# Two PSUM pools and the place of two groups of transposes in an attention and expert kernel

## The chip, the cores and the metric

The kernel runs on one core of a Trainium2 chip. The metric is the device time of one execution in microseconds (us). The core has five engines that work side by side and hand work to each other by semaphores: PE (matrix products and transposes, whose weight loads are shown apart as PEld), DVE and ACT (elementwise work; only these two empty PSUM here), POOL (elementwise work in SBUF and some DMA issues) and SP (DMA issues).

## The reference

Attention with local and global tokens, then a mixture of eight experts whose routing weights come from Sinkhorn steps. Shapes: 8 batches, 8 heads, 512 local and 32 global tokens, head size 64; D = 512, E = 8, F = 1024, N = 8 x 544 = 4352 rows.

```python
k_all, v_all = concat([k_g, k_l]), concat([v_g, v_l])
out_g = softmax(scale * q_g @ k_all.T) @ v_all              # global rows see everything
s_ll  = where(|i - j| <= 32, scale * q_l @ k_l.T, -1e9)     # local rows see a band ...
a_l   = softmax(concat([scale * q_l @ k_g.T, s_ll]))        # ... and the global keys
out_l = a_l @ v_all
x = concat([out_g, out_l]) as rows of 512
P = exp(x @ w_gate - max);  8 times: P /= rowsum; P /= colsum; P *= N / E
out = sum over e of  P[:, e] * (relu(x @ w1[e]) @ w2[e])
```

## The kernel before

The kernel has three stages. In the first, up to about 341 us, attention is worked off in slots, and the first products (`x @ w1`) of experts 0 to 3 are placed between its steps as fillers. Then come the Sinkhorn steps with the fillers that are left, and from about 376 us on the expert stage, which is not touched.

A unit of attention is a pair of heads of one batch: `HP` = 4 pairs, 8 batches, 32 units. The loop over `s` writes out one slot after the other; slot s works on scores of unit s and finishes unit s - 1. The order within a slot is the order in which the lines are written: every engine takes its own instructions in that order. Slots 0 to 3 are built differently; the loop in question runs from s = 4 to 32. Steps of a slot, with what each puts on the engines:

- `st_B(s, 0..2)`: scores of the eight blocks of unit s, in groups of three, three and two (PE, L299 and L301, tile `sc`); DVE adds the mask and takes the extreme value (L306, tile `ms`); ACT takes the exponential (L309, tile `Pu`).
- `st_N(s, ...)`: DVE takes reciprocals of the sums (L345) and normalises `Pu` (L346); POOL does the same for the columns of the global keys (L350, tile `Pl`).
- `st_D1(s - 1)`: eight transposes of the normalised `Pu` on PE (L357, tile `ptw`), copied to SBUF by DVE (L359, tile `pw`).
- `st_D2(s - 1)`: two transposes of `Pl` on PE (L365), copied by ACT (L367, tile `pg`).
- `st_A(s + 1)`: transposes of the next unit's keys and queries (PE, L273), copied by DVE (L274, `kTe`) and ACT (L283, `qbd`).
- `st_E(s - 1)`: probabilities times values (PE, L378 and L381, tile `po`), evicted from the ninth unit on by ACT (L384, `xT`).
- For global rows, two pairs of heads at a time: `st_G0` (POOL copies into `qgbd`), `st_G1` (PE, L407, tile `sg`; maximum on DVE, L409 and L410; exponential on ACT, L412, tile `Pg`), in the next slot `st_GN` (DVE, L418 and L419: reciprocal and normalisation of `Pg`), `st_G2` (five transposes on PE, L426, copied by ACT, L428, tile `pgs`) and `st_G3` (PE, L440 and L441, tile `pog`; ACT, L445). `st_G1` runs at the end of slots 5 to 8 and of the odd slots from 9 on; `st_GN`, `st_G2` and `st_G3` in the slots 6 to 9 and the even slots from 10 on.
- `f1("a")`, `f1("v")`: one filler each, four matmuls of 128 x 512 (PE, L466, tile `ph`), evicted by ACT (L469) or DVE (L471). `f1("va")` is two of them, the first evicted by DVE.
- `logits` in the slots 5, 9, 13 and so on: small products (PE, L453), copied by DVE (L455).

PSUM is divided into pools: `ps_mm` (two buffers, tag `mm`: fillers and logits), `ps_sc` (two, tag `sc`: scores and `pog`), `ps_po` (one, tag `po`, large enough for `sg`: `po` of `st_E` and `sg` of `st_G1` take turns) and `ps_tr` (two, tag `tr`: all the transposes). A tile waits for the readers of the tile that held its buffer before.

From slot 9 on, a slot before the change runs: D1, GN, G0, two fillers (`"aa"`), B0, D2, G2, B1, two fillers (`"va"`), A, B2, one filler (`"v"`), E, G3, two fillers (`"va"`), N, then in slots without G1 one filler (`"v"`), in some `logits`, and in odd slots G1.

Of the kernel before, what the change touches and what calls it, by code (L numbers as in the profile page):

```python
# [10 lines left out]
FP32 = mybir.dt.float32  # L11
# [12 lines left out]
def kernel(  # L24
# [15 lines left out]
    B, H, Sl, Dh = q_l.shape  # L40
# [3 lines left out]
    P = 128  # L44
# [6 lines left out]
    HP = H // 2  # L51
# [34 lines left out]
    ps_po = pss.enter_context(tc.tile_pool(name="ps_po", bufs=1, space=PSUM))  # L86
# [3 lines left out]
    with tc.tile_pool(name="att_c", bufs=1) as att_c, \  # L90
# [121 lines left out]
        def run(steps):  # L212
            for f in steps:
                f()
# [70 lines left out]
        def st_B(n, part):  # L285
            b, hp = divmod(n, HP)
            qb, kt = qbd[n % 2], kTe[n % NK]
            if part == 0:
                st[n] = dict(Pu=att_wk.tile([P, NHB, SW], FP16, tag="Pu", name="Pu"),
                             mx=att_wk.tile([P, NHB], FP32, tag="mx", name="mx"),  # L290
                             sm=att_wk.tile([P, NHB], FP32, tag="sm", name="sm"))
            d = st[n]
            i0 = 3 * part
            ni = min(3, NHB - i0)
            sc = ps_sc.tile([P, 512], FP32, tag="sc")
            ms = att_wk.tile([P, 3, SW], FP32, tag="ms")
            for ii in range(ni):
                i = i0 + ii
                nc.tensor.matmul(sc[:, SW * ii : SW * ii + KW], qb[:, i, :],  # L299
                                 kt[:, HB * i : HB * i + KW], start=True, stop=True)  # L300
                nc.tensor.matmul(sc[:, SW * ii + KW : SW * (ii + 1)], qb[:, i, :],  # L301
                                 kgT[:, hp, Sg * b : Sg * (b + 1)], start=True, stop=True)
            for ii in range(ni):
                i = i0 + ii
                mi = 0 if i == 0 else (2 if i == NHB - 1 else 1)
                nc.vector.tensor_tensor_reduce(  # L306
                    out=ms[:, ii, :], in0=sc[:, SW * ii : SW * (ii + 1)], in1=mask[:, mi, :],
                    scale=-scale, scalar=BIG, op0=ALU.add, op1=ALU.min, accum_out=d["mx"][:, i : i + 1])
                nc.scalar.activation(out=d["Pu"][:, i, :], in_=ms[:, ii, :], func=AF.Exp, scale=-1.0,  # L309
                                     bias=d["mx"][:, i : i + 1], accum_out=d["sm"][:, i : i + 1])  # L310
# [42 lines left out]
        def st_D1(n):  # L353
            d = st[n]
            ptw = ps_tr.tile([P, NHB, P], FP16, tag="tr")
            for i in range(NHB):
                nc.tensor.transpose(ptw[:, i, :], d["Pu"][:, i, 0:KW], identity)  # L357
            d["pw"] = att_wk.tile([P, NHB, P], FP16, tag="pw", name="pw")
            nc.vector.tensor_copy(out=d["pw"], in_=ptw)  # L359

        def st_D2(n):
            d = st[n]
            pt = ps_tr.tile([P, 2, P], FP16, tag="tr")
            for t in range(2):
                nc.tensor.transpose(pt[:, t, :], d["Pl"][:, 4 * t : 4 * t + 4, :], identity)  # L365
            d["pg"] = att_wk.tile([P, 2, P], FP16, tag="pg", name="pg")
            nc.scalar.copy(out=d["pg"], in_=pt)  # L367

        def st_E(n):
            b, hp = divmod(n, HP)  # L370
            d = st.pop(n)
            vz = vgz[b % 2]
            po = ps_po.tile([P, Sl], FP32, tag="po", name="po")
            for i in range(NHB):
                c = slice(HB * i, HB * (i + 1))
                halves = [(a, slice(HB * a, HB * (a + 1))) for a in range(2)]
                for a, r in halves:
                    nc.tensor.matmul(po[r, c], vab[b % 2][i % 2][:, i // 2, 2 * hp + a, :], d["pw"][:, i, r],  # L378
                                     start=True, stop=False)
                for a, r in halves:  # L380
                    nc.tensor.matmul(po[r, c], vz[:, i % 4, 2 * hp + a, :], d["pg"][:, i // 4, r],  # L381
                                     start=False, stop=True)
            cp = nc.vector.tensor_copy if HP <= n < 2 * HP else nc.scalar.copy
            cp(out=xT[b][:, hp, :], in_=po)  # L384
            if hp == HP - 1:
                nc.sync.dma_start(out=xd[b], in_=xT[b])
# [34 lines left out]
        def st_G2(b, g):  # L421
            Pg = gs[(b, g)][0]
            pt = ps_tr.tile([P, 5, P], FP16, tag="tr")
            for t in range(5):
                c0 = P * t if t < 4 else S - P
                nc.tensor.transpose(pt[:, t, :], Pg[:, c0 : c0 + P], identity)  # L426
            pgs = att_wk.tile([P, 5, P], FP16, tag="pgs", bufs=1)
            nc.scalar.copy(out=pgs, in_=pt)  # L428
            gs[(b, g)] = pgs
# [58 lines left out]
        def f1(engs, **kw):  # L488
            nonlocal n1
            v = 0  # L490
            for eng in engs:
                k, fm = divmod(n1, FT)
                if k < len(fill) and slot >= HP * fill[k][1] + 5:
                    p_l1(*fill[k], fm, eng, **kw)
                    n1 += 1
                    v += 1 if fill[k][1] < B else 0.5
            return v
# [75 lines left out]
        for s in range(HP, NU + 1):  # L573
            slot = s
            b, hp = divmod(s, HP)
            g1 = s in gat
            g23 = s - 1 in gat
            if g1:
                gn = divmod(gat[s], 2)
            if g23:  # L580
                gp = divmod(gat[s - 1], 2)
            if s == HP:
                st_B(s, 0)
                st_D1(s - 1)
                st_D2(s - 1)
                select_v(1, 0, range(2, NJ))
                st_E(s - 1)
                select_v(1, 1, (NJ - 1,))
                slot = s + 1
                va, vb = vab[1]  # L590
                nc.scalar.dma_start(out=vb[0:HB, 0 : NJ - 1], in_=va[HB:P, 0 : NJ - 1])
                nc.scalar.dma_start(out=vb[HB:P, 0 : NJ - 1], in_=va[0:HB, 1:NJ])
                cast_qk(1, 1, gq)
            else:
                if s <= 2 * HP:
                    st_B(s, 0)
                st_D1(s - 1)
                if g23:
                    st_GN(*gp)
            if g1 and s > HP + 1:  # L600
                st_G0(*gn)
            f1("aa")
            if 2 * HP < s < NU:
                st_B(s, 0)
            if s > HP:
                st_D2(s - 1)
            if g23:
                st_G2(*gp)
            if s < NU:
                st_B(s, 1)  # L610
            if s > HP:
                f1("va")
            if s + 1 < NU:
                st_A(s + 1)
            if s < NU:
                st_B(s, 2)
            f1("v")
            if s > HP:
                st_E(s - 1)
            if s == HP + 1:  # L620
                for t, (src, g, dst) in gcast:
                    transpose_g(t, g, dst)
                st_G0(*gn)
            if g23:
                st_G3(*gp)
            if s > HP:
                f1("va")
            if s < NU:
                st_N(s, 0, 6)
                st_N(s, 6, NHB)  # L630
            if s == HP:
                gcast = [(cast_g(x[0], x[1]), x) for x in ((kgf, 1, kgT), (qgf, 0, qgT), (qgf, 1, qgT))]
                load_w1e(3)
            if s > 2 * HP and not g1:
                f1("v")
            if s >= 5 and (s - 5) % HP == 0:
                logits(NJ * ((s - 5) // HP), NJ)
            if g1:
                st_G1(*gn)
            if s < NU and b + 1 < B:  # L640
                if hp == 0:
                    load_qk(b + 1, 0, (nc.sync, nc.sync))
                    load_qk(b + 1, 1, (nc.sync, nc.sync))
                elif hp == 1:
                    cast_qk(b + 1, 0, gq)
                    if b >= NL - 1:
                        load_w1d(b + 1)
                elif hp == 2:
                    vq = load_v(b + 1)
                    run(vq[:3])  # L650
                    cast_qk(b + 1, 1, gq)
                else:
                    run(vq[3:])
# [273 lines left out]
    for fm in range(FT):  # L927
        pool, tag = cyc[fm % 2]
# [10 lines left out]
    for i, (m, e) in enumerate(units):  # L939
        if i == NUN - 1:  # L940
            last_pair(i)
        elif i % 2 == 0:
# [9 lines left out]
            else:  # L952
                n = groups[m][1]
                h = hs[i + 1]
                s = ss[i + 1] = xsp.tile([P, HF, n], FP16, tag="xs", name="sl")
# [55 lines left out]
```

## Time and profile before

| what | value |
|---|---|
| median of 3 runs | 1057.38 us (1055.8 to 1061.52) |
| the profiled execution, its span | 1057.3 us, 1055.5 us |
| busy over the span: PE, PEld, DVE, ACT, POOL | 97%, 66%, 77%, 46%, 13% |
| busy in 95 to 331 us (236 us): PE, PEld, DVE, ACT, POOL | 229.59, 129.50, 180.44, 192.37, 72.70 us |
| busy in 376 to 1055 us (679 us): PE, DVE, ACT | 672.87, 527.60, 201.90 us |
| granted TensorE clock in 95 to 1055 us | 1.00 |

Times are us from the start of the span. A row of a timeline has the start, the duration, the engine, the line, the operation, the tiles written and read, their shapes and a count; what follows in square brackets is idle time of that engine ahead of the row and what ended it. A row of the waits names who waited for whom, the total, the number of times and the longest.

### The profile page before, as it was taken

To read this page: it belongs to the slowest core of one execution; us is meant where nothing else is said; L and a number is where in the kernel's file an instruction comes from. 1 tells how busy PE (TensorE), PEld (TensorE's weight loads), DVE (VectorE), ACT (ScalarE), POOL (GpSimd) and SP (SyncE) were. 2 spreads that over 40 slices of the span, in tenths; PEclk is the share of its full clock that TensorE was granted. 3 is DMA by queue.
4 is the path that set the end of the run, shared out by engine and by line. 5 is a ranking of instruction groups with operands and counts; after the bars stand their busy time and mean duration, and the time that the engine had idled before them with its cause. 6 is when DMAs were issued, how large, how long until landed. Compare 5 with 4: busy or idle time off the path is not lost.

```text
span 1055.5 us, 21693 instructions
## 1 busy us (share of the span) xinstructions
PE 1025.4 (97%) x8854; PEld 700.0 (66%) x8854; DVE 809.6 (77%) x1466; ACT 489.4 (46%) x1248; POOL 132.2 (13%) x215
## 2 busy tenths in 40 slices
PE   7799999999999999999999999999999999999998
PEld 4455555555554466677777777777777777777787
DVE  8587777777776776997877877778777787688685
ACT  7678888787886674222222223223223233132231
POOL 7441423413313002000000000000000000000000
PEclk9899999999999999999999999999999999999999
DMA  9887598987945999935435435335336435535441
GB/s 273 200 193 211 106 261 203 218 239 156 255 130 170 270 275 303 259 106 189 170 112 194 154 140 195 125 141 199 143 117 200 168 117 177 209 100 184 170 165 31
DMA packets 97348, 190.82 MB, mean 181 GB/s; under 512 B 33425, under 2 KB 63585, under 8 KB 84449
## 3 DMA queue, kind: packets, MB, share of 16 engines
q1 hardware_dynamic: 54208, 159.61, 43.6%
q0 software_dynamic: 40432, 20.20, 14.8%
q10 hardware_dynamic: 2608, 9.64, 2.4%
q8 instruction: 69, 1.13, 0.4%
q14 instruction: 31, 0.25, 0.1%
HBM read 157.11 MB, written 53.62 MB: 200 GB/s over the span
## 4 chain that ended last, share of the span: by engine, by line
PE 79%; DVE 9%; ACT 7%; issue 3%; DMA 1%; POOL 0%; ACTq 0%; SPq 0%; DVEq 0%; POOLq 0%
PE m L795 26%; PE ph L752 21%; PE ph L466 15%; PE pm L795 10%; ACT Pu L309 3%; DVE Pu L346 3%; PE ptw L357 1%; DVE h L672 1%; ACT hT L469 1%; PE pt L273 1%; ACT qbd L283 1%; DMA h<-hd 1%; PE po L378 1%; PE sc L299 1%; DVE m L409 1%
## 5 line engine op out<-in xcount | busy, mean ns | idle before, releaser
L754 ACT ACTIVATE h<-ph 128x512 f16<-128x512 f32 (+1 forms) x288 | 164.8, 573 | 405.9 <-PE ph L752 397.1
L752 PE MATMUL ph<-xs,w1s 128*128 128x512 f16 (+1 forms) x1152 | 269.4, 367 | 2.0 <-DVE o L811 2.0
L466 PE MATMUL ph<-xT,w1e 128*128 128x512 f16 (+1 forms) x1152 | 257.2, 368 | 0.2
L795 PEld LDWEIGHTS <-h 128*128 128x128 f16 x2144 | 209.8, 98 | 44.1
L795 PE MATMUL m<-w2c,s 128*128 128x256 f16 x1620 | 199.9, 273 | 0.0
L672 DVE TENSOR_TENSOR s<-h 128x1024 f16<-128x1024 f16 (+2 forms) x140 | 122.8, 919 | 91.2 <-ACT h L754 46.8
L795 PEld LDWEIGHTS <-s 128*128 128x128 f16 x1620 | 158.5, 98 | 38.2
L466 PEld LDWEIGHTS <-w1e 128*128 128x128 f16 x1152 | 105.6, 98 | 96.6 <-issue 4.5
L752 PEld LDWEIGHTS <-w1s 128*128 128x128 f16 x1152 | 112.7, 98 | 84.8 <-issue 2.3
L672 DVE TENSOR_TENSOR h<-h,pb 128x4096 f16<-128x4096 f16 (+1 forms) x35 | 148.3, 4237 | 3.1 <-DMA h<-hd 2.9
L795 PE MATMUL m<-w2c,h 128*128 128x256 f16 x1072 | 134.2, 273 | 0.0
L469 ACT ACTIVATE hT<-ph 128x512 f16<-128x512 f32 (+1 forms) x191 | 103.8, 558 | 47.5 <-PE ph L466 46.1
L795 PE MATMUL pm<-w2c,h 128*128 128x256 f16 x1072 | 122.9, 273 | 0.0
L672 DVE TENSOR_TENSOR xs<-xg,pb 128x2048 f16<-128x2048 f16 (+1 forms) x36 | 78.0, 2168 | 46.1 <-DMA pb<-pd 40.9
L309 ACT ACTIVATE Pu<-ms,mx 128x160 f16<-128x160 f32 x224 | 93.6, 420 | 3.9 <-DVE mx L306 1.5
L471 DVE TENSOR_SCALAR hT<-ph 128x512 f16<-128x512 f32 x97 | 66.8, 689 | 31.3 <-PE ph L466 30.6
L672 DVE TENSOR_TENSOR h<-h 128x1024 f16<-128x1024 f16 (+1 forms) x140 | 86.8, 661 | 0.0
L306 DVE CUSTOM_DVE_ANT_0 ms<-sc,mask 128x160 f32<-128x160 f32 x224 | 59.9, 320 | 24.5 <-PE sc L301 22.0
L350 POOL TENSOR_TENSOR Pl<-Pu,rs 128x256 f16<-128x256 f16 x32 | 24.7, 771 | 196.7 <-DVE rs L345 131.6
L811 DVE SCALAR_TENSOR_TENSOR o<-m,o 128x512 f32<-128x512 f32 (+1 forms) x72 | 43.3, 655 | 5.2 <-ACT o L809 3.5
L346 DVE TENSOR_TENSOR Pu<-Pu,rs 128x768 f16<-128x768 f16 x64 | 45.1, 705 | 2.2
L309 ACT ACTIVATION_READ_ACCUMULATOR Pu<-ms,mx 128x1 f32 x224 | 42.4, 189 | 0.0
(157 smaller groups left out, 903.7 us busy)
## 6 DMA issues: line engine op xcount, KB each, us to landing
w1s<-w1d SPq DMA_DIRECT2D x36, 1024.0 KB
h<-hd SPq DMA_DIRECT2D x32, 1024.0 KB
hd<-hT SPq DMA_DIRECT2D x26, 1024.0 KB
pb<-pd SPq DMA_DIRECT2D x64, 256.0 KB
w2c<-in_moe_w_dram POOLq DMA_DIRECT2D x16, 512.0 KB, 21.0
out_dram<-o SPq DMA_DIRECT2D x8, 1024.0 KB
f<-in_q_l_dram SPq DMA_DIRECT2D x15, 512.0 KB
f<-in_k_l_dram SPq DMA_DIRECT2D x15, 512.0 KB
```

The costliest lines, as they stand in the source:

```text
L306: nc.vector.tensor_tensor_reduce(out=ms[:, ii, :], in0=sc[:, SW * ii : SW * (ii + 1)], in1=mask[:, mi, :], scale=-scale, scalar=BIG, op0=A ...
L309: nc.scalar.activation(out=d["Pu"][:, i, :], in_=ms[:, ii, :], func=AF.Exp, scale=-1.0, bias=d["mx"][:, i : i + 1], accum_out=d["sm"][:, i ...
L346: nc.vector.tensor_tensor(out=d["Pu"][:, i0:i1, 0:KW], in0=d["Pu"][:, i0:i1, 0:KW], in1=d["rs"][:, i0:i1].unsqueeze(2).to_broadcast([P, i1 ...
L350: nc.gpsimd.tensor_tensor(out=d["Pl"], in0=d["Pu"][:, :, KW:SW], in1=d["rs"].unsqueeze(2).to_broadcast([P, NHB, Sg]), op=ALU.mult)
L466: nc.tensor.matmul(ph[:, 0:n], wts[e][:, dk, P * fm : P * (fm + 1)], xT[m][:, dk, :], start=(dk == 0), stop=(dk == DP - 1))
L469: nc.scalar.activation(out=hT[:, fm, 0:n], in_=ph[:, 0:n], func=AF.Relu)
L471: nc.vector.tensor_scalar(out=hT[:, fm, 0:n], in0=ph[:, 0:n], scalar1=0.0, scalar2=None, op0=ALU.max)
L672: nc.vector.tensor_tensor(out=out, in0=in0, in1=in1, op=op)
L752: nc.tensor.matmul(ph[:, 0:n], w1s[i][:, dk, P * fm : P * (fm + 1)], xss[i][:, dk, 0:n], start=(dk == 0), stop=(dk == DP - 1))
L754: nc.scalar.activation(out=hs[i][:, fm, 0:n], in_=ph[:, 0:n], func=AF.Relu)
L795: nc.tensor.matmul(pm[:, HD * t : HD * (t + 1)], lhs[0][:, k, lhs[1] + P * t : lhs[1] + P * (t + 1)], w[:, k, q - 1, :], start=(k == 0 and ...
L811: nc.vector.scalar_tensor_tensor(out=o, in0=p, scalar=sg / float(E), in1=o, op0=ALU.mult, op1=ALU.add)
```

## The change

From unit 8 on (slot 9, the tenth), `po` of `st_E` is taken from `ps_tr` and no longer from `ps_po`. From slot 9 on, `st_D1` stands behind the first of the two fillers `"aa"` and not ahead of both, while `st_GN` stays ahead of the fillers; and `st_G2` stands behind `st_B(s, 1)` and not ahead of it. Earlier slots keep their order. The number of instructions is the same on each engine.

```diff
@@ st_E
-            po = ps_po.tile([P, Sl], FP32, tag="po", name="po")
+            pool, tag = (ps_tr, "tr") if n >= 2 * HP else (ps_po, "po")
+            po = pool.tile([P, Sl], FP32, tag=tag, name="po")
@@ the loop over slots
             else:
                 if s <= 2 * HP:
                     st_B(s, 0)
-                st_D1(s - 1)
+                if s <= 2 * HP:
+                    st_D1(s - 1)
                 if g23:
                     st_GN(*gp)
             if g1 and s > HP + 1:
                 st_G0(*gn)
-            f1("aa")
+            f1("a")
+            if s > 2 * HP:
+                st_D1(s - 1)
+            f1("a")
             if 2 * HP < s < NU:
                 st_B(s, 0)
             if s > HP:
                 st_D2(s - 1)
-            if g23:
+            if g23 and s <= 2 * HP:
                 st_G2(*gp)
             if s < NU:
                 st_B(s, 1)
+            if g23 and s > 2 * HP:
+                st_G2(*gp)
             if s > HP:
                 f1("va")
```

## The prediction

> **What bounds the kernel now.** I read the stage windows first, then the waits by engine, then the timelines of one pair of slots. Slots (`s`) count from 0, so the tenth is s = 9; s = 9 to 32 lie at about 94 to 341 us. Two slots, an odd and an even one, make a repeating pair. The windows view over two such pairs, the second with an `logits` call in it:
>
> ```profile
> 157.20:177.60 20.40, 19.76 (x213) 11.04 (x213) 15.60 (x56) 16.64 (x54) 9.00 (x14) 1.00 0.84 171
> 177.60:198.30 20.70, 20.23 (x229) 11.50 (x229) 15.86 (x57) 16.89 (x54) 4.94 (x9) 1.00 0.96 273
> ```
>
> Columns: stretch, length, busy time of PE, PEld, DVE, ACT, POOL, then clock and DMA. PE is busy for 19.8 of 20.4 us, but ACT has only 3.8 us free and DVE 4.8, so neither can fall far behind. The waits of PE and PEld in 130 to 370 us, in the view of the waits:
>
> ```profile
> PEld L357 <- DVE Pu L346: 8.2, 21, 0.6
> ...
> PE sg L407 <- ACT xT L384: 1.8, 4, 0.5
> ...
> PE pt L426 <- DVE Pg L419: 1.1, 5, 0.2
> ```
>
> These are the change's three targets: transposes of probabilities (L357, `st_D1`) wait for DVE's normalisation; global scores (L407, `st_G1`) wait for `st_E`'s eviction on ACT, since both use the one `po` buffer; transposes of global probabilities (L426, `st_G2`) wait for Pg. Matmul records overlap by about 0.2 us, so I take a gap as the next start less the last start less that matmul's stream (four fillers go out in 0.86 us, 0.215 each). In the pair without `logits` the gaps over 0.12 us are 0.23 + 0.28 (odd D1), 0.61 (sg), 0.19 (even D1) and 0.12 (G2): 1.43 us. With `logits` they are 0.23, 0.28, 0.13, 0.19, 0.39: 1.22 us. From s = 10 on they sum to 15.1 us.
>
> Now the even slot behind sg, s = 16, first on PE, then on DVE, then on ACT (timelines):
>
> ```profile
> 166.56 0.61 PE L407 MATMUL sg<-kTe,qgbd 128*128 128x480 f16 x4 [0.45 <-ACT xT L384]
> ...
> 169.99 0.45 PE L426 MATMUL pt<-identity,Pg 128*128 128x128 f16 x5
> ```
>
> ```profile
> 165.29 0.69 DVE L471 TENSOR_SCALAR hT<-ph 128x512 f16<-128x512 f32 x1 [0.84 <-PE ph L466]
> ...
> 167.52 0.72 DVE L409 TENSOR_REDUCE m<-sg 128x1 f32<-128x544 f32 x1
> 168.27 0.15 DVE L410 TENSOR_SCALAR m<-m 128x1 f32<-128x1 f32 x1
> 168.34 0.68 DVE L359 COPY pw<-ptw 128x1024 f16<-128x1024 f16 x1
> 169.36 0.16 DVE L418 RECIPROCAL m<-m 128x1 f32<-128x1 f32 x1 [0.34 <-ACT Pg L412]
> 169.56 0.37 DVE L419 TENSOR_SCALAR Pg<-Pg,m 128x544 f16<-128x544 f16 x1
> 169.94 0.33 DVE L306 CUSTOM_DVE_ANT_0 ms<-sc,mask 128x160 f32<-128x160 f32 x1
> ```
>
> ```profile
> 168.52 0.71 ACT L412 ACTIVATE Pg<-sg,m 128x544 f16<-128x544 f32 x1 [1.51 <-DVE m L410]
> ...
> 169.22 1.08 ACT L469 ACTIVATE hT<-ph 128x512 f16<-128x512 f32 x2
> 170.37 0.43 ACT L309 ACTIVATE Pu<-ms,mx 128x160 f16<-128x160 f32 x1
> ...
> 177.26 0.60 ACT L469 ACTIVATE hT<-ph 128x512 f16<-128x512 f32 x1
> ```
>
> To be seen: DVE runs without a gap from 165.29 to 168.42, so `m` does not start at 167.52 because sg was late. Its copy of the transposed probabilities (pw, L359) fills the time in which it would wait for ACT's Pg. And ACT runs without one idle interval from 168.52 to 177.86: no row in between names a releaser. The waits of ACT in 134 to 300 us have two lines only, L469 on PE and L412 on `m`.
>
> **The change part by part.** No instruction is added or removed; PE streams the same. Let x be the start of the two fillers ahead of sg in an odd slot (164.21 in s = 15; the next is 184.63, a period of 20.42).
>
> *PSUM of `st_E`.* sg no longer waits for xT: PE gains 0.61 or 0.13 per pair at that point. `m` still starts at x + 3.31, because DVE gets to it only then. So the gain is time in which PE is early, and it is kept only if nothing later waits. In return `po` takes turns with all the transposes in two buffers, and each now waits for the reader of the tile two before: in an even slot D1, D2, G2, A, E stand in that order, so E waits for the pgs copy (L428) and the next D2 for xT.
>
> *D1 behind a filler.* In odd slots D1's 0.51 goes, since the filler's 0.86 covers the normalisation. But that first filler is now the first thing in the slot, and takes the `mm` buffer of the filler two before, whose eviction is ACT's last in the even slot: L469, 177.26 + 0.60 = 177.86. PE's fillers had ended at about 177.42. So without any other effect 0.51 is exchanged for 0.44 to 0.5. Before, D1 stood in between and the filler started at 178.38, 0.52 after that eviction: that slack is what disappears.
>
> *What moved with it.* The change leaves `st_GN` where it was and puts D1 behind it, so on DVE pw now stands behind L418 and L419. DVE takes its work in written order in both kernels. It idles from 168.42 to 169.36 for ACT's Pg, normalises until 169.94, and only then copies pw (0.61 from start to start). Behind pw are queued the masked scores (L306) of B0, and ACT's exponentials wait for these. First L306: 169.94 + 0.61 = 170.55 instead of 169.94; the first Pu 0.41 later, 170.96 instead of 170.37: 0.59 later. This is a term the change does not intend, and nothing hides it, because ACT has no idle time behind it.
>
> *G2 behind B1.* PE arrives at D2 and B1 early and does them first, then waits for Pg, which is ready at 169.94 as before. It gets there at x + 0.86 x 2 + 0.56 (sg) + 0.86 + 0.45 (D1) + 0.86 + 0.25 + 0.11 + 0.25 = x + 5.06 to 5.1 and waits 0.65. B1's 0.25 is won on PE. On ACT pgs moves behind B1's three exponentials; the sum of its work stays the same.
>
> *The pair summed.* Before: ACT's Pu start x + 6.16; ACT's stretch up to the last eviction 177.86 - 170.37 = 7.49, all back to back, with the same instructions in both kernels. After: Pu start x + 6.75; last eviction x + 14.24; filler + D1 + filler 0.86 + 0.45 + 0.86 = 2.17, and scores B0 of the odd slot at x + 16.45 to 16.5. Before, these started at 180.11 = x + 15.90. From B0 to the next x PE has 4.5 us without a wait in both (180.11 to 184.63): ACT's and DVE's rows of the odd slot lie as far behind B0 as before. The loss is 0.60 per pair. PE's waits in between (G2 0.65, A 0.5 for pg, E 0.3 for pgs, first filler 0.7) all fall in time that ACT needs anyway.
>
> With `logits`: x = 184.63, Pg ready at 190.61, Pu start before 190.94 = x + 6.31, after 190.61 + 0.61 + 0.41 = 191.6 = x + 6.97. B0 comes at 6.97 + 7.49 + 0.05 + 2.17 = x + 16.68, before at x + 16.15: 0.53.
>
> Slot 9 has both G2 and G1, and slot 10 again G2. From x = 91.96 by the same rows: Pu 98.69 instead of 98.19, and E, which waits for pgs, at 102.07 instead of 101.54; x of slot 10 is 0.53 late. By the `logits` sum the odd slot 11 then is 1.06 late. Ten more pairs (s = 11 to 30), five of each kind: 5 x 0.60 + 5 x 0.53 = 5.65. Slots 31 and 32 have no scores behind pw; G2 there is bound by Pg (333.82 = x + 5.76) before and after: 0. The filler that is left, the Sinkhorn steps and the expert stage come behind unchanged. Sum: +6.7 us.
>
> The profiled execution took 1057.3 us (span 1055.5 and 1.8 around it), the median of the runs is 1057.38: both the same here. 1057.3 + 6.7 = 1064.0.
>
> **Bounds of what the trace does not show.** The wait of the first filler on ACT does not occur in the trace. If it cost nothing the pair would gain at most its gaps, 1.43 and 1.22; if ACT's 7.49 also got a wait of its own (a late A or E), each one costs up to 0.5, the size of E's wait. I take 0: by the sums A is released 5 us and E 2.5 us ahead of ACT's need for them.
>
> **Rivals.** *Faster: the gaps are PE's and go away.* The Trainium skill's Perfetto Trace Analysis, Identifying the Most-Contended Engine and Optimization Strategy, says to optimise the engine with the highest occupancy first, and that a repeating bubble on it can mean that PSUM is short; by that rule this change attacks the right place. The same page holds matmul busy time to be a bad measure of how near PE is to its limit; PEld, at 11.0 of 20.4 us here, is far from full. As a mechanism here: sg, D1 and G2 start when PE arrives, and ACT and DVE follow since they have 3.8 and 4.8 us free per pair. All gaps gone: 1057.3 - 15.1 = 1042; half of them 1050. For it: 97% PE. Against: ACT's free time lies ahead of Pg and in the odd slots' beginning, not behind Pu. Chance 0.17.
>
> *No change: pw's place costs nothing.* If the first Pu still starts at x + 6.16, the filler goes at x + 13.73 and B0 at x + 15.90, exactly as before: gained and lost waits cancel, 1057 (1053 to 1062). This decides if something else on ACT ended 0.6 us later anyway; its evictions end at 170.30, so I see nothing. Chance 0.23, with smaller values of my own sum in it.
>
> *Much slower: the shared transpose buffers become the bound.* E and A wait for ACT's copies, and the next sum is late by A's 0.5 and E's 0.3 in each pair on top: 12 x 0.8 = 9.6, so 1074. It decides once A's or E's wait outlasts ACT's stretch. For it: five tiles in two buffers. Against: 2.5 us of slack. Chance 0.10.
>
> **How the numbers follow.** The forecast, 1060 to 1069, has 0.50; rivals 0.17, 0.23, 0.10. About 0.5% (5.3 us) is what a measurement of this kernel can tell from no change. Of the forecast about a tenth of the weight lies below +5.3, so slower is 0.46 + 0.10 = 0.56, same 0.04 + 0.23 = 0.27, faster 0.17. The range takes in the no-change case and the beginning of both outer ones: 1052 to 1073, leaving out about 0.13 below and 0.07 above. The forecast's own range is 1060 to 1069.
>
> **What would show it.** After the change, the pair lasts about 21.0 us, not 20.4. sg's wait for xT and D1's for Pu are gone from PE's waits; instead PE waits for ACT L469 in front of the first filler of odd slots (0.6 to 0.7 us, 10 to 12 times), for Pg at G2 (0.65) and for pg and pgs. On DVE the wait of L418 for Pg grows from 0.34 to about 0.94, and pw stands behind L419. ACT waits about 0.6 for DVE in front of the even slots' first Pu. I am wrong if the pairs get shorter than 20.4, or if ACT shows no wait at that Pu.

## The result and the profile after

The changed kernel takes 1065.54 us (median of 6 runs, 1063.64 to 1068.17) against 1058.7 us before (6 runs); the ratio is 1.007 (95% interval 1.0055 to 1.0084). It is slower, by about the 6.7 us forecast. The profiled execution has a span of 1063.9 us.

The first slots, in which both kernels do the same, differ between profiled executions: `st_E` of slot 8 started at 91.03 us before and at 93.47 after. I therefore compare the stretch from the first matmul of `st_E` in slot 8 to that in slot 32 (PE's timeline): 336.87 - 91.03 = 245.84 us before, 345.55 - 93.47 = 252.08 after, **+6.24 us**. What follows slot 32 takes the same, 718.6 and 718.3 us.

The windows view of one pair without and one with `logits`, cut at the first filler of odd slots (columns as before: stretch, length, busy time of PE, PEld, DVE, ACT, POOL):

```profile
161.92:182.79 20.87, 19.35 (x214) 11.26 (x214) 15.49 (x56) 16.76 (x53) 8.99 (x15) 1.00 0.77 151
182.79:203.93 21.14, 19.86 (x230) 11.70 (x230) 15.77 (x57) 16.76 (x53) 4.94 (x10) 1.00 0.91 262
```

The pairs last 20.87 and 21.14 us, where they lasted 20.4 and 20.7; the busy times of DVE and ACT are within 0.13 us of those before, and PE's is about 0.4 less. So the time is waiting. The waits of all engines in 130 to 370 us:

```profile
...
PE pt L427 <- DVE pw L359: 11.2, 11, 1.6
DVE m L419 <- ACT Pg L413: 10.3, 11, 0.9
...
ACT Pu L309 <- DVE mx L306: 6.2, 10, 0.7
...
PE ph L467 <- ACT hT L470: 3.0, 10, 0.3
...
```

(Behind `st_E` the new lines count one or more higher: L413 is L412 before, L419 and L420 are L418 and L419, L427 is L426, L467 and L470 are L466 and L469.) The waits that the change aimed at, of sg for xT and of D1 for Pu, are gone. In their place DVE waits 0.93 us for Pg (0.34 before), ACT waits 0.6 us for DVE ahead of the even slots' first Pu, where it had no wait before, and PE waits at G2, and in odd slots for ACT's last eviction. The even slot that answers to the one shown before, on PE, DVE and ACT (timelines; x is 168.61):

```profile
170.34 0.61 PE L408 MATMUL sg<-kTe,qgbd 128*128 128x480 f16 x4
...
174.97 0.44 PE L427 MATMUL pt<-identity,Pg 128*128 128x128 f16 x5 [1.10 <-DVE pw L359]
...
182.79 1.02 PE L467 MATMUL ph<-xT,w1e 128*128 128x512 f16 x4 [0.30 <-ACT hT L470]
```

```profile
172.66 0.15 DVE L411 TENSOR_SCALAR m<-m 128x1 f32<-128x1 f32 x1
173.75 0.16 DVE L419 RECIPROCAL m<-m 128x1 f32<-128x1 f32 x1 [0.93 <-ACT Pg L413]
173.95 0.37 DVE L420 TENSOR_SCALAR Pg<-Pg,m 128x544 f16<-128x544 f16 x1
174.24 0.67 DVE L359 COPY pw<-ptw 128x1024 f16<-128x1024 f16 x1
174.84 0.31 DVE L306 CUSTOM_DVE_ANT_0 ms<-sc,mask 128x160 f32<-128x160 f32 x1
```

```profile
175.25 0.43 ACT L309 ACTIVATE Pu<-ms,mx 128x160 f16<-128x160 f32 x1 [0.56 <-DVE mx L306]
...
182.14 0.60 ACT L470 ACTIVATE hT<-ph 128x512 f16<-128x512 f32 x1
```

To be seen: the transposes for pw ended at 172.41 (171.71 + 0.70 on PE) and DVE was free at 172.8, but the copy stands behind the wait for Pg until 174.24. The first Pu starts at x + 6.64 and not at x + 6.16; ACT then runs 182.74 - 175.25 = 7.49 us without a gap, as before; and PE's next filler starts at 182.79, 0.05 behind ACT's last eviction. It does so in every odd slot from 11 on, and by the starts of the matmuls PE had been ready 0.46 us earlier each time.

### The profile page after: what moved, and what is told of

Same layout as the page of the kernel before. It is cut to its first block, busy times and chain, and to the rows that moved or that the text cites. A ratio compares the mean times of both kernels' runs of the same rounds, so it can differ in the third digit from the quotient of the medians.

```text
span 1063.9 us, 21693 instructions
## 1 busy us (share of the span) xinstructions
PE 1022.1 (96%) x8854; PEld 703.1 (66%) x8854; DVE 809.7 (76%) x1466; ACT 489.6 (46%) x1248; POOL 131.5 (12%) x215
## 4 chain that ended last, share of the span: by engine, by line
PE 69%; ACT 15%; DVE 9%; DMA 4%; issue 2%; SPq 0%; POOL 0%; ACTq 0%; DVEq 0%; POOLq 0%
PE m L802 26%; PE ph L759 21%; PE pm L802 10%; PE ph L467 9%; ACT Pu L309 7%; ACT hT L470 2%; DVE Pu L346 2%; ACT qbd L283 2%; DVE h L679 1%; DMA vgz<-vg 1%; DMA vg<-in_v_g_dram 1%; DVE m L410 1%; DMA h<-hd 1%; ACT Pg L413 1%; DVE pw L359 1%
## 5 line engine op out<-in xcount | busy, mean ns | idle before, releaser
L467 PE MATMUL ph<-xT,w1e 128*128 128x512 f16 (+1 forms) x1152 | 261.3, 368 | 3.8 <-ACT hT L470 3.5
L467 PEld LDWEIGHTS <-w1e 128*128 128x128 f16 x1152 | 105.3, 98 | 99.1 <-issue 10.9
L470 ACT ACTIVATE hT<-ph 128x512 f16<-128x512 f32 (+1 forms) x191 | 103.8, 559 | 46.7 <-PE ph L467 44.5
```

The lines of the kernel that those rows point to most:

```text
L467: nc.tensor.matmul(ph[:, 0:n], wts[e][:, dk, P * fm : P * (fm + 1)], xT[m][:, dk, :], start=(dk == 0), stop=(dk == DP - 1))
L470: nc.scalar.activation(out=hT[:, fm, 0:n], in_=ph[:, 0:n], func=AF.Relu)
```

## The experiments

My theory was the order on DVE: pw behind the wait for Pg delays the stretch on ACT that has no slack. The rivals were the shared transpose buffers, the filler in front of D1, and PE's gaps being worth their length. Every ratio is against the kernel before; the stretch is that from slot 8 to slot 32, of one profiled execution.

| kernel | ratio (95%) | stretch, us |
|---|---|---|
| before | | 245.84 |
| the change | 1.007 (1.0055 to 1.0084) | 252.08 |
| e1, GN behind D1 | 0.998 (0.9965 to 0.9995) | 244.28 |
| e2, change without PSUM part | 1.0055 (1.0035 to 1.0074) | 251.83 |
| e3, PSUM part alone | 1.0014 (0.9998 to 1.0031) | 245.82 |
| e4, GN ahead of D1 alone | 1.0078 (1.0056 to 1.0101) | 253.37 |
| e5, G2 moved alone | 0.9983 (0.9971 to 0.9995) | 243.72 |
| e6, e1 and xT on DVE | 0.9936 (0.9916 to 0.9955) | 239.79 |
| e7, path shortened | 0.9924 (0.9903 to 0.9944) | 237.39 |
| e8, e7 without PSUM part | 0.9938 (0.9919 to 0.9957) | 238.10 |
| e9, two buffers by reader | 0.9871 (0.985 to 0.9892) | 232.28 |

**e4, the swap alone.** The kernel before, with two lines exchanged:

```diff
-                st_D1(s - 1)
+                if s <= 2 * HP:
+                    st_D1(s - 1)
                 if g23:
                     st_GN(*gp)
+                if s > 2 * HP:
+                    st_D1(s - 1)
```

> The kernel before with one swap alone: from slot 9 on st_GN stands ahead of st_D1, both ahead of the two fillers; PSUM, fillers and G2 as before. Theory: pw stands behind the wait for Pg, G2 takes the buffer that pw frees and starts about 0.55 later in even slots, ACT's first Pu too; 13 slots with 0.5 to 0.6 us each: 6 to 7.5 us, ratio 1.006 to 1.007. Rivals (buffers, or the filler in front of D1): neither is in this kernel, so ratio 0.999 to 1.001.

The stretch grew by 253.37 - 245.84 = 7.53 us, 0.58 for each of 13 slots (9 and the even ones from 10 to 32), with no instruction more and no other step moved. ACT's and PE's waits in 134 to 306 us:

```profile
...
ACT Pu L309 <- DVE mx L306: 5.1, 8, 0.7
```

```profile
PE pt L426 <- DVE pw L359: 5.5, 8, 0.8
...
```

The same two new waits as in the changed kernel. The swap by itself costs what the whole change costs, and a little more. But the delay is passed on by another way (three rows of PE's timeline and one of ACT's; x is 168.48):

```profile
174.84 0.44 PE L426 MATMUL pt<-identity,Pg 128*128 128x128 f16 x5 [0.55 <-DVE pw L359]
...
182.49 0.90 PE L357 MATMUL ptw<-identity,Pu 128*128 128x128 f16 x8
183.22 1.89 PE L466 MATMUL ph<-xT,w1e 128*128 128x512 f16 x8
```

```profile
182.01 0.60 ACT L469 ACTIVATE hT<-ph 128x512 f16<-128x512 f32 x1
```

ACT's first Pu is as late as in the changed kernel (x + 6.64). But PE's next filler starts 0.61 us behind ACT's last eviction (182.01 + 0.60), about as far as before (0.51 to 0.63), so ACT does not hold it up. From G2 to the next D1 PE takes 7.65 us, and 7.66 before. So in e4 it is PE that passes the delay on: it waits at G2 for the buffer that pw's copy frees. In the changed kernel, where D1 no longer stands between, it is ACT.

**e1, the change without the swap.**

```diff
                 if s <= 2 * HP:
                     st_D1(s - 1)
-                if g23:
+                if g23 and s <= 2 * HP:
                     st_GN(*gp)
...
             if s > 2 * HP:
                 st_D1(s - 1)
+                if g23:
+                    st_GN(*gp)
             f1("a")
```

> The changed kernel with st_GN put behind st_D1 from slot 9 on, so that DVE copies pw before it waits for Pg; the PSUM pool, the filler and G2 stay as changed. Theory (the copy of pw stands behind the wait for Pg and delays ACT's unbroken stretch): the even slots' first Pu falls back to x + 6.16, L418/L419 wait about 0.34 for Pg and not 0.94, G2 waits for Pg and no longer for pw, the pair is 20.4 us again and the time within 2 us of before (ratio 0.998 to 1.002). Rival (the shared transpose buffers cost it): G2, A and E still wait for buffers, the pair stays near 20.9 and the ratio near 1.006. Rival (the first filler of odd slots behind ACT's last eviction costs it, whatever DVE does): 1.004 to 1.006.

The loss is gone, and the rest of the change is worth 0.2%: 245.84 - 244.28 = 1.56 us. PE's waits in 134 to 306 us:

```profile
PE pt L427 <- DVE Pg L420: 3.1, 8, 0.5
PE ph L467 <- ACT hT L470: 2.7, 9, 0.3
```

G2 waits for Pg and no longer for pw, and ACT no longer waits for DVE ahead of the first Pu, which starts at x + 6.04 (x is 164.01; one row of DVE's timeline and one of ACT's):

```profile
168.14 0.68 DVE L359 COPY pw<-ptw 128x1024 f16<-128x1024 f16 x1
```

```profile
170.05 0.43 ACT L309 ACTIVATE Pu<-ms,mx 128x160 f16<-128x160 f32 x1
```

PE still waits for ACT's last eviction in front of odd slots, 0.46 us by the starts of the matmuls: the rival of the filler is right that this wait exists, but it only stands where D1's wait stood.

**e2 and e3, the PSUM part taken away and alone.** e2 is the changed kernel with `po = ps_po.tile(...)` as before, e3 the kernel before with the two new lines for `po`.

> The changed kernel with the outputs of st_E back in their own PSUM pool; the two moved groups of transposes stay. Theory: sg waits for xT again (0.6 or 0.1 us on PE) but DVE reaches its maximum no later, E no longer waits 0.28 for pgs, and neither lies on the path through DVE and ACT: ratio 1.005 to 1.007, as the whole change. Rival (shared transpose buffers are the cost): back to 1.000 to 1.002. Rival (the PSUM part gains its PE gaps of 3.7 us and hides a larger loss): 1.009 to 1.011.

> The kernel before with the PSUM part alone: outputs of st_E from the transposes' pool, no step moved. Theory: sg starts 0.6 or 0.1 us earlier, but DVE reaches its maximum no later or earlier than before, so D1 and G2 wait that much longer: ratio 0.999 to 1.001, sg's wait gone and G2's wait for Pg grown. Rival (gaps on PE are worth their length): 3.7 us, ratio 0.9965.

e2 stays slower: 251.83 against 252.08 us in the stretch, and its ratio does not differ from the change's by more than the intervals allow. By the starts of `st_E` each pair is 0.46 us longer than before in both. e3 is the clearest case. sg starts earlier and its wait is gone, and what PE waits for in 134 to 306 us is now

```profile
PE ptw L357 <- DVE Pu L346: 2.1, 4, 0.5
PE pt L427 <- DVE Pg L420: 0.2, 1, 0.2
```

The time that PE idled in front of sg appears behind it, in front of D1 (PE's timeline). By the starts of the matmuls it is 0.61 us in both places; the rows name 0.45 before and 0.52 here:

```profile
165.02 0.61 PE L408 MATMUL sg<-kTe,qgbd 128*128 128x480 f16 x4
165.48 0.20 PE L408 MATMUL sg<-kgT,qgbd 128*128 128x32 f16 x2
166.20 0.90 PE L357 MATMUL ptw<-identity,Pu 128*128 128x128 f16 x8 [0.52 <-DVE Pu L346]
```

The stretch moved by 0.02 us. The rival's 3.7 us of gaps in front of sg were worth nothing. The ratio is just over the expected range, with an interval that reaches into it. G2's wait did not grow as expected, it is 0.09 us shorter: D1 alone took over the time.

**e5, G2 alone.** The kernel before with `st_G2` behind `st_B(s, 1)` from slot 9 on, as in the change's diff.

> The kernel before with G2 alone moved behind the second group of scores from slot 9 on. Theory: PE does B1 (0.25 us) while it would wait for Pg; the even slots' fillers behind it start 0.2 to 0.25 us earlier, D1 of the odd slots too, and the fillers after D1 still come behind ACT's last eviction: the pair 20.15 to 20.25, 12 pairs, 2 to 3 us faster, ratio 0.997 to 0.998. Rival (PE's gaps are all bound by ACT's stretch, so that nothing moved on PE counts): 1.000.

It is faster, at the lower end of what was expected: 2.12 us. By the starts of `st_E`, pairs with `logits` gain 0.25 us and those without it 0.12. By the starts of the matmuls PE waited 0.39 and 0.12 us at G2 before; behind B1 it waits 0.14 with `logits`, and without it not at all. So these gaps on PE were worth what the move filled of them. Together with e4 this says that in the kernel before it was the chain of work through PE that held the pair, and not ACT's stretch. e5 alone gains more than e1 (2.12 against 1.56 us in the stretch): what the other two parts cost there, 0.56 us, was not tried by itself.

**e6, ACT's stretch made shorter.** e1, and in `st_E`:

```diff
-            cp = nc.vector.tensor_copy if HP <= n < 2 * HP else nc.scalar.copy
+            cp = nc.vector.tensor_copy if HP <= n < 2 * HP or n > 2 * HP and n % 2 else nc.scalar.copy
```

> e1 (the change with st_GN behind st_D1) and one eviction more on DVE: xT of the even slots from slot 10 on. Theory: what is left in e1 is PE's wait of 0.46 for ACT's last eviction in front of odd slots; ACT's stretch gets 0.48 shorter (7.0 and not 7.49) and DVE idles over 1 us at that point, so 0.3 to 0.46 per pair on top of e1: ratio 0.993 to 0.995. Rival (PE alone is the bound now): as e1, 0.998. Rival (DVE has no room): over 1.000.

One eviction of 0.59 us moved from ACT to DVE in each even slot takes 4.49 us off e1's stretch, 0.4 per pair. PE's wait for ACT's eviction is gone; of e1's two waits in the same window one is left:

```profile
PE pt L427 <- DVE Pg L420: 3.1, 8, 0.5
```

This shows that ACT's stretch was the bound of the pair in e1, which the page's 46% for ACT does not tell.

**e7 and e8, the path ahead of the stretch made shorter.** e6, and:

```diff
+            early = s > 2 * HP and s % 2 == 1
+            if early:
+                st_N(s, 0, 6)
+                st_N(s, 6, NHB)
             if s > HP:
                 f1("va")
-            if s < NU:
+            if s < NU and not early:
...
+            if early:
+                st_G1(*gn)
             if s >= 5 and (s - 5) % HP == 0:
                 logits(NJ * ((s - 5) // HP), NJ)
-            if g1:
+            if g1 and not early:
                 st_G1(*gn)
```

and in even slots D1 and GN ahead of the fillers. e8 is the same with `po` in its own pool.

> e6, and the path from the odd slots' fillers to the even slots' first Pu shortened: in odd slots st_N stands ahead of the last two fillers, so that DVE's maximum of sg comes at x + 2.9 and not 3.3; logits stand behind st_G1; in even slots st_D1 and st_GN stand ahead of the fillers as before. Theory: the first Pu at about x + 5.65 and not 6.16, ACT's stretch 7.0, B0 of the odd slot near x + 14.9 and not 15.9: 0.8 to 1.0 us per pair against before, ratio 0.989 to 0.992. Rival (PE's own stream of 18.7 to 19 us is reached, or the first filler of even slots waits for the eviction that now stands behind st_N): 0.993 to 0.995, no better than e6.

> e7 with the outputs of st_E back in their own pool. Theory: sg again waits for xT to x + 2.35, ends 0.2 us behind DVE's arrival at the maximum, and now lies on the path: 0.2 to 0.3 per pair slower than e7, ratio 0.991 to 0.995. Rival (the PSUM part never matters): as e7.

e7 lies between the two expectations. By the starts of `st_E`, pairs without `logits` gain 1.0 us against before, as the theory says, and pairs with it only 0.43: there the products of `logits` take the buffer of a filler whose eviction now stands behind `st_N` (PE's waits, 130 to 370 us):

```profile
PE pl L454 <- DVE hT L472: 3.4, 6, 0.6
...
```

e8's ratio is in its range but cannot be told from e7's; its stretch is 0.71 us longer, 0.06 per pair and not 0.2 to 0.3. By the starts of `st_E` that mean hides two kinds: pairs without `logits` are 0.23 us slower than in e7, as expected, and pairs with it 0.07 faster. In the latter PE waits at sg, ahead of the products of `logits`, and of the wait for their buffer 0.14 us is left.

**e9, both buffers by their readers.**

```diff
-            pool, tag = (ps_tr, "tr") if n >= 2 * HP else (ps_po, "po")
+            pool, tag = (ps_tr, "tr") if n >= 2 * HP and n % 2 == 0 else (ps_po, "po")
...
-            pl = ps_mm.tile([P, 512], FP32, tag="mm")
+            pool, tag = (ps_sc, "sc") if 2 * HP < slot < NU else (ps_mm, "mm")
+            pl = pool.tile([P, 512], FP32, tag=tag, name="pl")
```

> e7 with two PSUM buffers chosen by their readers: st_E takes the transposes' pool in odd slots only (there sg follows it) and its own pool in even slots, and the products of logits take the scores' pool and not the fillers'. Theory: in e7 PE waits 0.26 in every even slot for pgs, whose buffer st_E takes, and 0.72 in the slots with logits for the eviction of the filler two before; both waits go, 12 x 0.26 + 6 x 0.72 = 7.4 us, and nothing else ends later: ratio 0.985 to 0.987. Rival (the path through DVE and ACT to the first Pu takes its place): half of it or less, 0.989 to 0.992.

1044.84 us (4 runs), 0.9871 of the kernel before, and 13.56 us less in the stretch; 5.1 us of the 7.4 expected came, and the ratio is just above the range, with an interval that holds it. By the starts of `st_E` nearly all of it came in the pairs with `logits`, 0.82 us each against e7; those without gained 0.07, so that the gap of 0.26 us ahead of E in even slots was worth little (0.09 of it stands ahead of E in every slot, before the change too). PE's waits in 95 to 345 us are down to

```profile
PE pt L427 <- DVE Pg L420: 0.7, 2, 0.5
PE pl L455 <- DVE hT L473: 0.4, 1, 0.4
PE ph L468 <- DVE hT L473: 0.2, 1, 0.2
```

This version beats both kernels.

## Why the prediction was right

The forecast was 1064.0 us and +6.7; measured were 1065.54 against 1058.7 us, and +6.24 in the stretch.

*What moved with it.* Shown by e4 and e1: the swap of pw and GN, which the change does not name, carries the whole loss. The path that I forecast, through ACT's stretch to the odd slot's first filler, is the one in the rows of the changed kernel; e4 alone would not show it, because there PE passes the delay on. L419's wait for Pg is 0.93 (forecast 0.94). The first Pu came 0.48 late and not 0.59: pw started 0.29 behind the start of L420 and not 0.38, so this term was too large by 0.1.

*The pair.* Forecast 0.60 and 0.53, measured 0.46 for both kinds: 4.63 us over the ten pairs from slot 10 to 30, not 5.65. B0 of the odd slot came at 184.96 = x + 16.35, forecast x + 16.45 to 16.5. By its own terms my sum gives 0.56 for the first kind (x + 16.46 against x + 15.90), and I wrote 0.60; the term of 0.1 above accounts for the rest.

*G2 behind B1: the step that was wrong.* I had G2 wait 0.65 us for Pg. In the pairs it waits 0.8 to 1.25 us (starts of the matmuls) for pw: D1, D2 and G2 follow each other in two buffers, so G2 takes the one that pw's copy frees. I had written that order down and drawn from it what E and the next D2 wait for, but not this. It had two effects. In the pairs it cost nothing, because ACT was later anyway, by 0.46 us; A then came late enough not to wait for pg, so the 0.5 us given for A did not occur. In slot 32, where no scores follow, I had put 0; there the wait counted in full, 0.57 us.

*Slots 9 and 10.* Forecast 0.53 and 1.06 in all by slot 11; measured 0.52 in slot 9, 1.09 by slot 10, 1.03 by slot 11.

*D1 behind a filler, and the PSUM part.* As forecast: D1's and sg's waits went, the first filler of odd slots waits for ACT (0.46 us by the starts of the matmuls, forecast 0.7: ACT's last eviction came 0.1 earlier, and PE, held up at G2, came later), the gap ahead of E is 0.28 (forecast 0.3; 0.09 of it stood there before). The sum was right in part by balance: about 1.0 too much in the pairs, 0.57 too little in slot 32.

*The rivals.* The faster one fell by the result, and for the gap in front of sg by e3: its 0.61 us, taken away, were waited out in front of D1. It was right for the gap at G2, which e5 turned into 2.12 us. The Trainium skill's Perfetto Trace Analysis (Identifying the Most-Contended Engine) says to optimise the engine of highest occupancy first, and not to judge PE's headroom by its matmul busy time but by MFU (the share of the peak rate that the matmuls reach) and the share of its weight loads. In 95 to 331 us of the kernel before, matmuls were busy 97% of the time, weight loads 55%, ACT 82%. Work taken from ACT gained 4.49 us on top of e1 (e6), the gap on PE in front of sg nothing (e3), the one at G2 2.12 us (e5). So the shares did not tell which of PE's gaps counted, and matmul busy time alone would have passed over ACT. The rival of no change has its place decided by e1: without the swap, gained and lost waits cancel up to 1.56 us. Sharing the transposes' buffers with `po` never became the bound (e2).

## What to carry to other kernels

When a step is moved behind another, look at every engine that it has work on: here a copy that was ready fell behind an instruction that waits for a third engine, and that one exchange cost 7.5 us by itself (e4), where the rest of the change gained 1.6 (e1). The same delay can be passed on by different engines in two versions of a kernel, so the path has to be read anew in each. A gap on the busiest engine is worth something only if its end is what the next late thing waits for; follow the path to the next stretch that runs without a gap, and shorten that. And when a tile changes its pool, write down for each tile of the pool whose reader frees its buffer, in the new order, for all of them.

## What the runs showed of the hardware

The start of the program is not steady: `st_E` of slot 8 began between 90.11 and 93.47 us in eleven profiled executions in which everything up to there is the same, while the stretch behind it seems to repeat closely: the kernel before and e3 took 245.84 and 245.82 us, within 0.02 us of each other at every slot. No kernel was profiled twice, so this is not shown for one and the same kernel. By these numbers a difference of 2 us between two spans here says little, and one between two such stretches more.

DVE's normalisation of Pg (L419 before, L420 after) takes 0.36 to 0.37 us in slots from 9 on where POOL runs no cast, and 0.54 where POOL runs one (L129) at the same time, which is so in slots 10, 14, 18, 22 and 26, before and after. In slot 7 it takes 0.60 with no cast beside it, while POOL issues DMAs (L182). What they share was not tested.
